# Banded attention inside a gated layer, forward and backward: score and gradient products as 32-row matmuls

## The chip, the cores and the metric

The kernel runs on one core of one Trainium2 chip. The metric is the time of one execution on the device in microseconds, lower is better. The times of before are three runs; the profile is one further execution of the same program, recorded by the hardware profiler. Engines are named as in the profile: PE is TensorE (its weight loads are listed apart, as PEld), DVE is VectorE, ACT is ScalarE, POOL is GpSimd, SP is SyncE, which here only issues transfers.

## The reference

Two branches read the same rows x (2048 x 512, bf16): attention with 32 heads of 16 channels in which each query sees the 256 keys up to its own, and a gated ReLU network of 1376 hidden channels. A sigmoid gate g of x mixes them. The kernel returns the output and the gradients of x and of every weight, for a given gradient of the output.

```python
def _A_ref(x, wqkv, wo):
    H = 32; Dh = D // H; W = 256
    q, k, v = ...                              # (x @ wqkv), split into heads
    scores = einsum("bhqd,bhkd->bhqk", q, k) * (Dh ** -0.5)
    mask = (idx[:, None] - idx[None, :] >= 0) & (idx[:, None] - idx[None, :] < W)
    p = softmax(where(mask, scores, -1e9))
    o = einsum("bhqk,bhkd->bhqd", p, v)
    return o.reshape(B, S, D) @ wo

def _fwd_reference(...):
    g = sigmoid((x * gate_w).sum(-1, keepdims=True))
    return g * _A_ref(x, A_wqkv, A_wo) + (1 - g) * _B_ref(x, B_W_gate, B_W_up, B_W_down)

out, vjp = jax.vjp(f, A_x, A_wqkv, A_wo, B_W_gate, B_W_up, B_W_down, gate_w)
return (out, *vjp(grad_out))
```

## The kernel before

Three stages follow each other. The first (0 to 259 us) makes the gated network's forward and weight gradients; the second (to about 777 us) is the attention, forward and backward; the third makes the output rows and the gradient of x. The change is in the second, with a little preparation in the first.

**Layout.** 512 channels are four column blocks c of 128, so a block has eight heads of 16 channels. 2048 positions are 16 tiles of 128, in four groups of four. For each block and group `project_parts` (L119) makes Q, dO, K and V transposed: channels on the 128 partitions, 512 positions along the row. Q and dO go into the tile `zT` (L136). K and V are each written twice (`K0`, `K1`, `V0`, `V1`, L153 to L160), multiplied by a 0/1 column `par`, so that `K0` keeps the even heads of each pair and has zeros for the odd ones, and `K1` the other way round. A pair of heads is 32 partitions, a strip; a block has four strips.

**The padded operand.** `zt` (L108) holds Q and dO again, as [128, 2, 4 tiles, 4 strips, 128]: for strip k only the partitions 32k to 32k+31 are filled, everything else is zero. It is cleared once at the end of the first stage (L443 to L446) and filled for the first group by eight copies (L145 to L151), later by four transfers per group, `spread` (L468), issued on SP: 64 KB each.

**Units.** A unit (L624 to L640) is one block c, one query tile j, one key tile kb (j, j-1 or j-2: roles d, m, f) and one `half`, which is the parity of the heads it treats, four heads. There are 360. Within a query tile the units of half 0 come first, then those of half 1. The score product ST (`front`, L643, matmul L649) multiplies `K{half}` of the key tile with the four padded copies of the query tile: 128 rows, 128 columns of weights, 512 moving columns, giving four heads' scores with keys on partitions, in one PSUM bank. ACT takes the exponential into `Pu` (L655), POOL masks it by role d or f (L657, L660). The gradient product dPT (`front_dp`, L663, matmul L669) does the same with `V{half}` and dO. DVE multiplies `Pu` with dPT into `Pd` (`gradp`, L671, L674).

**What follows a unit.** `rowsum` (L676) sums into BA with eight small matmuls; `flip` (L694) transposes `Pu` and `Pd`, either by a transfer on SP (159 units, their pair is the tile `PP`) or by eight PE transposes into a PSUM tile `pt` (L706) that ACT and DVE copy out in turn (L72, L74; 201 units). `cd_piece` (L480) uses the flipped tiles for the gradients of K and V (L488, L491). `small_ops` (L711) gives POOL seven small products per query tile.

**Order.** The loop at L821 writes the order out by hand; the framework adds the waits but moves nothing. In step n: POOL's small products; `front` of unit n (ST, exponential, mask); `gradp` of unit n-1; transposing transfers of n-2; `rowsum` and `flip` of n-3; `front_dp` of unit n; pieces of CD; then at most one piece of background, a part of the next group's projection (`prq`) or of the previous block's weight gradients (`bgq`, `grad_parts`, L557), if a running `credit` allows. The credit grows per step by `SLOT` less fixed charges (L872).

**PSUM.** Eight banks: tag "M" has four for ST, dPT, projection sums `pp` and weight-gradient sums `wps`; "TR" two for transposes; one each for CD and BA. A `wps` sum keeps its bank over four background pieces (`held`).

Of the kernel before, what the change touches and what calls it, by code (L numbers as in the profile page):

```python
# [22 lines left out]
def kernel(  # L23
# [21 lines left out]
    P = 128  # L45
# [67 lines left out]
    if True:  # L113
# [5 lines left out]
        def project_parts(c, tg):  # L119
# [4 lines left out]
            def mm(nm, which, eng):  # L124
                ps, tag, bufs, _ = pools["now"]
                pp = ps.tile([P, TGW], F32, tag=tag, bufs=bufs, name="pp")
# [7 lines left out]
                if nm in ("Q", "dO"):  # L134
                    if nm == "Q":
                        t4["z"] = pjA.tile([P, 2, TGW], BF, tag="zT", name="zT")  # L136
                    dst = t4["z"][:, ("Q", "dO").index(nm), :]
                else:
                    dst = pjA.tile([P, TGW], BF, tag="T", bufs=2, name=f"{nm}T")[:]
# [4 lines left out]
                t4[nm] = dst  # L144
                if nm in ("Q", "dO"):  # L145
                    if c == 0 and tg == 0:
                        w = ("Q", "dO").index(nm)
                        for k in range(NP):
                            rows = slice(32 * k, 32 * k + 32)
                            evac(zt[0][rows, w, :, k, :], dst[rows, :].rearrange("p (k q) -> p k q", k=TPG),  # L150
                                 (("dve", "act")[w] if k % 2 else "dve"))  # L151
                else:
                    for k in range(2):  # L153
                        t4[f"{nm}{k}"] = pj.tile([P, TGW], BF, tag=f"{nm}{k}", name=f"{nm}{k}")
                        if PENG[k] == "act":
                            nc.scalar.mul(t4[f"{nm}{k}"][:], pp[:], par[:, k:k + 1])
                        elif PENG[k] == "dve":
                            nc.vector.tensor_scalar(t4[f"{nm}{k}"][:], pp[:], par[:, k:k + 1], None, op0=ALU.mult)
                        else:
                            nc.vector.tensor_scalar(t4[f"{nm}{k}"][:], dst[:], par[:, k:k + 1], None, op0=ALU.mult)  # L160

            def tr(a_nm, b_nm):
                ps, tag, bufs, trt = pools["now"]
                pt = ps.tile([P, 2, TPG, P], BF, tag=trt, bufs=2, name="ptp")
                for a, nm in enumerate((a_nm, b_nm)):
                    for k in range(TPG):
                        nc.tensor.transpose(pt[:, a, k, :], t4[nm][:, k * P:(k + 1) * P], ident[:])
                return pt
# [20 lines left out]
    with ExitStack() as p1, tc.manual_schedule():  # L189
# [209 lines left out]
        DA0 = 2 * NTG  # L399
        pools["now"] = (ps1, "tr", 2, "tr")  # L400
        first = []
        turn_x(0)
        stores = {}
        for n in range(N1 + 8):
# [36 lines left out]
            if n == NTG + 1:  # L441
                nc.scalar.activation(tiny[:], tiny[:], ACT.Exp)
            if t in (NT + 3, NT + 5):  # L443
                i = (t - NT - 3) // 2
                nc.gpsimd.memset(zt[i][:, 0, :, :, :], 0.0)
                nc.vector.memset(zt[i][:, 1, :, :, :], 0.0)  # L446
            if n == N1 - 2:
# [11 lines left out]
    if True:  # L459
# [6 lines left out]
        ps = pps.enter_context(tc.tile_pool(name="attps", bufs=2, space=PSUM))  # L466
        pools["now"] = (ps, "M", 4, "TR")
        def spread(gi, k):  # L468
            rows = slice(32 * k, 32 * k + 32)
            nc.sync.dma_start(zt[gi % ZB][rows, :, :, k, :],  # L470
                              proj[groups[gi]]["z"][rows, :, :].rearrange("p w (k q) -> p w k q", k=TPG))

        P2 = {}
# [6 lines left out]
        def cd_piece(c, kb, qb, half, last):  # L480
# [5 lines left out]
            for hh in range(HH):  # L486
                h = 2 * hh + half
                nc.tensor.matmul(cd[0][:, h, :], lhsT=p2[:, 0, hh, :], rhs=rq[:, h, 0:2 * Dh],  # L488
# [51 lines left out]
        def load_wo():  # L540
            t = pjA.tile([P, 2, TGW], BF, tag="zT", name="wo_z")
            for k in range(2):
                load_rows("wo", A_wo, k, t[:, k, :])
            for k in range(2, DC):
                load_rows("wo", A_wo, k, pjA.tile([P, TGW], BF, tag="T", bufs=2, name="wo_t")[:])
# [11 lines left out]
        def grad_parts(c, rest=None):  # L557
# [22 lines left out]
            def piece(part, t0, first, last):  # L580
                if first:
                    tag, bufs = ("TR", 2) if part == DC and rest is not None else ("M", 4)
                    hold[part] = ps.tile([P, 3, P] if part < DC else [P, D], F32, tag=tag, bufs=bufs, name="wps")
                wps = hold[part]
                for t in range(t0, t0 + 4):
                    go_, no_ = first and t == t0, last and t == t0 + 3
                    if part < DC:
                        nc.tensor.matmul(wps[:], lhsT=x_r[:, t, part * P:(part + 1) * P], rhs=sts[c][:, t, 0:3, :],  # L588
                                         start=go_, stop=no_)
                    else:  # L590
                        nc.tensor.matmul(wps[:], lhsT=sts[c][:, t, 3, :], rhs=rows[t], start=go_, stop=no_)
                if not last:
                    return None
                if part < DC:
                    ws = (gwp if rest is None else S2["t6"]).tile([P, 3, P], BF, tag="ws", bufs=2 if rest is None else 5, name="ws")
                    evac(ws[:], wps[:], "act" if rest is None or part % 2 else "dve")
                    return store(part, ws)
                if t0 + 4 < NT:
                    hold["half"] = gwp.tile([P, D], F32, tag="half", bufs=1, name="half")
                    evac(hold["half"][:], wps[:], "act")  # L600
                    for k in range(4, 8):
# [3 lines left out]
                if "half" in hold:  # L605
                    nc.vector.tensor_tensor(out=ws[:], in0=hold["half"][:], in1=wps[:], op=ALU.add)
                else:
                    evac(ws[:], wps[:], "act")
                return store(part, ws)
# [31 lines left out]
        NU = len(units)  # L641

        def front(u):  # L643
            tg, jl = u.j // TPG, u.j % TPG
            z = zt[(u.c * NTG + tg) % ZB]
            KTt = proj[(u.c, u.kb // TPG)][f"K{u.half}"]
            ksl = slice((u.kb % TPG) * P, (u.kb % TPG + 1) * P)
            ST = ps.tile([P, HH, P], F32, tag="M", bufs=4, name="ST")
            nc.tensor.matmul(ST[:], lhsT=KTt[:, ksl], rhs=z[:, 0, jl, :, :], start=True, stop=True)  # L649
            if u.dma or u.role == "d":  # L650
                u.PP = wk.tile([P, 2, HH, P], BF, tag="PP", bufs=5, name="PP")
                u.Pu, u.Pd = u.PP[:, 0, :, :], u.PP[:, 1, :, :]
            else:
                u.Pu = wk.tile([P, HH, P], BF, tag="Pu", bufs=3, name="Pu")
            nc.scalar.activation(u.Pu[:], ST[:], ACT.Exp)  # L655
            if u.role == "d":
# [5 lines left out]

        def front_dp(u):  # L663
            tg, jl = u.j // TPG, u.j % TPG
            z = zt[(u.c * NTG + tg) % ZB]
            VTt = proj[(u.c, u.kb // TPG)][f"V{u.half}"]
            ksl = slice((u.kb % TPG) * P, (u.kb % TPG + 1) * P)
            u.dPT = ps.tile([P, HH, P], F32, tag="M", bufs=4, name="dPT")
            nc.tensor.matmul(u.dPT[:], lhsT=VTt[:, ksl], rhs=z[:, 1, jl, :, :], start=True, stop=True)  # L669

        def gradp(u):  # L671
            if u.role != "d" and not u.dma:
                u.Pd = wk.tile([P, HH, P], BF, tag="Pd", bufs=3, name="Pd")
            nc.vector.tensor_tensor(out=u.Pd[:], in0=u.Pu[:], in1=u.dPT[:], op=ALU.mult)  # L674

        def rowsum(u):  # L676
# [4 lines left out]
            for hh in range(HH):  # L681
                h = 2 * hh + u.half
                nc.tensor.matmul(BA[:, h, 0:33], lhsT=u.Pu[:, hh, :], rhs=kv[:, u.kb % TPG, h, 1:34],  # L683
# [10 lines left out]
        def flip(u):  # L694
# [7 lines left out]
            copier["i"] += 1  # L702
            pt = ps.tile([P, 2, HH, P], BF, tag="TR", name="pt")
            for a, src in enumerate((u.Pu, u.Pd)):
# [95 lines left out]
        with tc.manual_schedule():  # L800
# [4 lines left out]
            credit = 1.2  # L805
            SLOT = 1.5
            LAG = 3
# [13 lines left out]
            while n <= NU + LAG or ev or cdq or bgq:  # L821
# [5 lines left out]
                if u is not None:  # L827
# [13 lines left out]
                    if u.first and u.j == TPG - 1 and u.c > 0:  # L841
                        bgq += ready
                    front(u)
                    if u.last and gi + 1 == len(groups) and u.j % TPG in (1, 3):
# [8 lines left out]
                if LAG <= n < NU + LAG:  # L853
# [4 lines left out]
                    if w.last:  # L858
# [5 lines left out]
                        for kb in done:  # L864
                            qbs = range(kb, min(NT, kb + 3))
                            for qb in qbs:
                                for half in range(2):
                                    e = n + 1 if qb < w.j else n + 5
                                    cdq.append((e, w.c, kb, qb, half, qb == qbs[-1] and half == 1))
                if u is not None:  # L870
                    front_dp(u)
                credit += SLOT - 0.63 - (0.44 if LAG <= n < NU + LAG and not units[n - LAG].dma else 0.0)  # L872
                for _ in range(2 if len(cdq) > 6 or (len(cdq) > 1 and cdq[1][5] and cdq[1][0] <= n and cdq[1][2] < NT - 1) else 1):
# [13 lines left out]
                elif prq and not held and (credit > 0.4 or due - n <= len(prq)):  # L887
                    credit -= (0.44, 0.86, 0.86, 0.1, 0.86, 0.86)[len(prq) - 1]
                    prq.pop(0)()
                    if len(prq) == 4:  # L890
                        for k in range(NP):
                            ev.setdefault(n + 1 + k // 2, []).append(("dma", lambda gi=gi, k=k: spread(gi + 1, k)))
                    if not prq:
# [134 lines left out]
```

## Time and profile before

| | us |
|---|---|
| median of three runs | 968.75 (966.98 to 973.46) |
| the profiled execution | 971.04 |
| its span, first to last instruction | 969.0 |
| granted TensorE clock, share of full speed | 0.994 |

Busy times over the span, with the number of instructions:

| engine | busy us | share | instructions |
|---|---|---|---|
| PE | 938.9 | 97% | 11281 |
| PEld | 598.3 | 62% | 11281 |
| DVE | 501.5 | 52% | 918 |
| ACT | 473.8 | 49% | 811 |
| POOL | 488.4 | 50% | 936 |

The groups that the change touches, as busy us in all and mean ns of one:

| line | what | count | busy us | mean ns |
|---|---|---|---|---|
| L649 | score product ST on PE | 360 | 136.8 | 380 |
| L669 | gradient product dPT on PE | 360 | 137.2 | 381 |
| L655 | exponential on ACT (both tiles) | 360 | 217.3 | 597 to 657 |
| L657, L660 | mask on POOL | 240 | 152.3 | 634 |
| L674 | product Pd on DVE (both tiles) | 360 | 245.0 | 681 |
| L706 | transposes into pt on PE | 1608 | 156.1 | 220 |
| L72 | copy of pt on ACT | 103 | 105.1 | 1020 |
| L74 | copy of pt on DVE | 102 | 69.5 | 681 |

Busy times of PE are the union of records that overlap, so a mean times a count is more than the busy time. The share over the whole span is an average over three stages. "Idle before" of a group is time in which its engine stood still ahead of it, with what ended the wait.

### The profile page before, as it was taken

The numbers are of one execution on the slowest core, as the hardware profiler recorded it, in microseconds if no ns is written. First come the engines' busy times: TensorE is split into PE (matmuls) and PEld (weight loads), VectorE is DVE, ScalarE is ACT, GpSimd is POOL, SyncE is SP. The second block draws the span as 40 slices with busy tenths as digits, with TensorE's granted clock in tenths as the row PEclk, the third lists the DMA queues.
The fourth block names the chain that finished last, engine by engine and source line by source line (L and its number), as shares of the span: only waits on it lengthen the run. The fifth ranks groups of instructions, "written<-read, shape, count | busy, mean of one in ns | idle before, by whom it ended". The sixth has DMA issues, their size and how long they took to land.

```text
span 969.0 us, 27638 instructions
## 1 busy us (share of the span) xinstructions
PE 938.9 (97%) x11281; PEld 598.3 (62%) x11281; DVE 501.5 (52%) x918; ACT 473.8 (49%) x811; POOL 488.4 (50%) x936
## 2 busy tenths in 40 slices
PE   7999999999999999999999999989999999999998
PEld 4556555656567777676776677756777754444443
DVE  4443323323377777666776667765667613223322
ACT  5422322222378777667776667766677720001001
POOL 2644345444177667666676556665657622121211
PEclk9999999999999999999999999998999999999999
DMA  9988899996667598985889857899999969866760
GB/s 291 185 201 206 218 218 210 220 196 174 143 114 122 100 160 155 154 146 100 145 126 189 138 103 139 127 162 175 160 141 229 185 184 260 194 171 165 183 155 28
DMA packets 447415, 161.64 MB, mean 167 GB/s; under 512 B 365784, under 2 KB 444984, under 8 KB 447288
## 3 DMA queue, kind: packets, MB, share of 16 engines
q1 hardware_dynamic: 424888, 136.80, 73.8%
q10 hardware_dynamic: 20592, 17.84, 6.1%
q0 software_dynamic: 1808, 5.24, 1.5%
q8 instruction: 88, 1.44, 0.7%
q14 instruction: 39, 0.32, 0.1%
HBM read 38.44 MB, written 38.41 MB: 79 GB/s over the span
## 4 chain that ended last, share of the span: by engine, by line
PE 82%; DMA 6%; POOL 4%; SPq 2%; DVE 2%; ACT 1%; issue 1%; ACTq 0%; POOLq 0%; DVEq 0%
PE pt L706 9%; PE dxps L970 8%; PE ST L649 7%; PE dPT L669 7%; PE wps L373 6%; PE wps L588 4%; PE dxps L991 4%; PE BA L683 4%; PE pp L129 4%; PE bps L941 4%; PE CD L488 4%; PE dhps L326 3%; PE ups L326 3%; PE dps L375 3%; PE gps L326 3%; PE CD L491 2%
## 5 line engine op out<-in xcount | busy, mean ns | idle before, releaser
L674 DVE TENSOR_TENSOR Pd<-Pu,dPT 128x512 bf16<-128x512 bf16 x201 | 136.6, 681 | 64.9 <-POOL Pu L660 53.5
L655 ACT ACTIVATE Pu<-ST 128x512 bf16<-128x512 f32 x201 | 121.6, 606 | 58.9 <-PE ST L649 57.3
L649 PE MATMUL ST<-z,K 128*128 128x512 bf16 x360 | 136.8, 380 | 4.0 <-DVE Pd L674 1.7
L669 PE MATMUL dPT<-z,V 128*128 128x512 bf16 x360 | 137.2, 381 | 1.3 <-DVE Pd L674 1.1
L674 DVE TENSOR_TENSOR PP<-PP,dPT 128x512 bf16<-128x512 bf16 x159 | 108.4, 682 | 41.0 <-POOL PP L657 38.1
L657 POOL TENSOR_SCALAR_AFFINE_SELECT PP<-PP 128x512 bf16<-128x512 bf16 x128 | 81.3, 635 | 79.5 <-ACT PP L655 78.8
L655 ACT ACTIVATE PP<-ST 128x512 bf16<-128x512 f32 x159 | 95.7, 602 | 51.7 <-PE ST L649 42.0
L340 POOL TENSOR_TENSOR hT<-rg,upm 128x512 bf16<-128x512 bf16 x44 | 52.2, 1186 | 123.9 <-DVE upm L338 98.4
L488 PE MATMUL CD<-rq,p 128*128 128x32 bf16 x1440 | 109.7, 177 | 0.8 <-ACT rows_st L494 0.5
L373 PE MATMUL wps<-dgu_r,x_r 128*128 128x256 bf16 x704 | 105.6, 272 | 4.9 <-DVE wst L74 4.9
L491 PEld LDWEIGHTS <-p 128*128 128x128 bf16 x1440 | 86.4, 96 | 35.9 <-issue 3.1
L72 ACT COPY p<-pt 128x1024 bf16<-128x1024 bf16 x103 | 105.1, 1020 | 5.2 <-PE pt L706 2.5
L491 PE MATMUL CD<-rq,p 128*128 128x16 bf16 x1440 | 106.7, 169 | 0.0
L488 PEld LDWEIGHTS <-p 128*128 128x128 bf16 x1440 | 99.0, 96 | 1.7 <-issue 1.5
L660 POOL TENSOR_SCALAR_AFFINE_SELECT Pu<-Pu 128x512 bf16<-128x512 bf16 x112 | 71.0, 634 | 41.8 <-ACT Pu L655 40.1
L373 PEld LDWEIGHTS <-x_r 128*128 128x128 bf16 x704 | 68.8, 98 | 36.7 <-issue 6.3
L948 ACT COPY a_sb<-aps 128x512 f32<-128x512 f32 x16 | 9.4, 585 | 145.8 <-issue 133.1
L706 PE MATMUL pt<-ident,Pd 128*128 128x128 bf16 x804 | 78.4, 220 | 0.0
L706 PE MATMUL pt<-ident,Pu 128*128 128x128 bf16 x804 | 77.7, 219 | 0.0
L74 DVE COPY p<-pt 128x1024 bf16<-128x1024 bf16 x102 | 69.5, 681 | 6.1 <-PE pt L706 5.4
L332 ACT ACTIVATE rg<-gps 128x512 bf16<-128x512 f32 x44 | 26.3, 598 | 91.0 <-PE gps L326 49.6
L683 PE MATMUL BA<-KV,Pu 128*128 128x33 bf16 x804 | 66.6, 178 | 4.1 <-ACT BAs L689 4.0
(158 smaller groups left out, 1998.7 us busy)
## 6 DMA issues: line engine op xcount, KB each, us to landing
dqkvo_d<-rows_st SPq DMA_DIRECT2D x7, 1024.0 KB, 5.7
dar<-da_d SPq DMA_DIRECT2D x28, 256.0 KB, 4.3
hT_d<-hT ACTq DMA_DIRECT2D x44, 128.0 KB, 2.4
dgT_d<-dgu ACTq DMA_DIRECT2D x44, 128.0 KB, 2.8
duT_d<-dgu ACTq DMA_DIRECT2D x44, 128.0 KB, 2.8
duT_g<-duT_d SPq DMA_DIRECT2D x8, 640.0 KB, 5.2
dgT_g<-dgT_d SPq DMA_DIRECT2D x7, 640.0 KB, 9.1
gt<-hT_d SPq DMA_DIRECT2D x7, 640.0 KB, 5.7
```

The lines of the kernel that those rows point to most:

```text
L72: nc.scalar.copy(out, in_)
L326: nc.tensor.matmul(out[:], lhsT=w(c), rhs=x(c), start=(c == 0), stop=(c == DC - 1))
L373: nc.tensor.matmul(acc["w"][:, c, :], lhsT=x_r[:, t, c * P:(c + 1) * P], rhs=k.dgu_r[:, :, i, :], start=(go_ and c % 2 == 0), stop=no_, sk ...
L488: nc.tensor.matmul(cd[0][:, h, :], lhsT=p2[:, 0, hh, :], rhs=rq[:, h, 0:2 * Dh], start=cd[1], stop=True, skip_group_check=True)
L491: nc.tensor.matmul(cd[0][:, h, 0:Dh], lhsT=p2[:, 1, hh, :], rhs=rq[:, h, 2 * Dh:3 * Dh], start=False, stop=True, skip_group_check=True)
L649: nc.tensor.matmul(ST[:], lhsT=KTt[:, ksl], rhs=z[:, 0, jl, :, :], start=True, stop=True)
L655: nc.scalar.activation(u.Pu[:], ST[:], ACT.Exp)
L657: nc.gpsimd.affine_select(out=u.Pu[:], in_=u.Pu[:], compare_op=ALU.is_ge, fill=0.0, base=0, pattern=[[0, HH], [1, P]], channel_multiplier=-1)
L669: nc.tensor.matmul(u.dPT[:], lhsT=VTt[:, ksl], rhs=z[:, 1, jl, :, :], start=True, stop=True)
L674: nc.vector.tensor_tensor(out=u.Pd[:], in0=u.Pu[:], in1=u.dPT[:], op=ALU.mult)
L683: nc.tensor.matmul(BA[:, h, 0:33], lhsT=u.Pu[:, hh, :], rhs=kv[:, u.kb % TPG, h, 1:34], start=(u.first and hh == 0), stop=True, skip_group ...
L706: nc.tensor.transpose(pt[:, a, hh, :], src[:, hh, :], ident[:])
```

## The change

Unit, half and strip get another meaning: `half` now names two neighbouring strips (partitions 0 to 63 or 64 to 127 of a block) in place of the parity, so that head `2*hh + half` becomes `HH*half + hh` in `rowsum` and `cd_piece`. A unit's scores are four matmuls of 32 rows, two strips by two parities, each 128 moving columns; so are its gradients. The moving operand is `zT` itself, unpadded. The scores of unit n and the gradients of unit n-1 are written together at the head of step n, strip by strip, and `front_dp` at the end of the step is gone. Scores and gradients of one unit share one PSUM tile `SD` of two banks, one bank per strip: within a bank two quarters hold scores and two hold gradients. There are two such tiles, in the place of the four banks of "M". The projection and weight-gradient sums move to the two banks of the transposes, now called "tr" (the last block's weight gradients, after the loop of units, go in pairs into "M"). `spread`, the padding, the clearing and the first copies are gone; `zT` has two buffers. `SLOT` is 1.4 in place of 1.5, and the fixed charge of the products 0.53 in place of 0.63.

```diff
-                        t4["z"] = pjA.tile([P, 2, TGW], BF, tag="zT", name="zT")
+                        t4["z"] = pjA.tile([P, 2, TGW], BF, tag="zT", bufs=2, name="zT")
...
-                if nm in ("Q", "dO"):
-                    if c == 0 and tg == 0:
-                        w = ("Q", "dO").index(nm)
-                        for k in range(NP):
-                            rows = slice(32 * k, 32 * k + 32)
-                            evac(zt[0][rows, w, :, k, :], dst[rows, :].rearrange("p (k q) -> p k q", k=TPG),
-                                 (("dve", "act")[w] if k % 2 else "dve"))
-                else:
+                if nm in ("K", "V"):
...
-        pools["now"] = (ps, "M", 4, "TR")
-        def spread(gi, k):
-            rows = slice(32 * k, 32 * k + 32)
-            nc.sync.dma_start(zt[gi % ZB][rows, :, :, k, :],
-                              proj[groups[gi]]["z"][rows, :, :].rearrange("p w (k q) -> p w k q", k=TPG))
-
+        pools["now"] = (ps, "tr", 2)
...
-                h = 2 * hh + half
+                h = HH * half + hh
...
-                if first:
-                    tag, bufs = ("TR", 2) if part == DC and rest is not None else ("M", 4)
-                    hold[part] = ps.tile([P, 3, P] if part < DC else [P, D], F32, tag=tag, bufs=bufs, name="wps")
+                if first and rest is not None and part < DC:
+                    if part % 2 == 0:
+                        hold["two"] = ps.tile([P, 2, TGW], F32, tag="M", bufs=2, name="wps")
+                    hold[part] = hold["two"][:, part % 2, 0:3 * P].rearrange("p (a n) -> p a n", a=3)
+                elif first:
+                    hold[part] = ps.tile([P, 3, P] if part < DC else [P, D], F32, tag="tr", bufs=2, name="wps")[:]
...
+        def score(u, nm, w, at, par):
+            tg, jl = u.j // TPG, u.j % TPG
+            lhs = proj[(u.c, u.kb // TPG)][f"{nm}{par}"]
+            z = proj[(u.c, tg)]["z"]
+            ksl = slice((u.kb % TPG) * P, (u.kb % TPG + 1) * P)
+            return [lambda i=i: nc.tensor.matmul(u.SD[:, i, at + par, :], lhsT=lhs[32 * (2 * u.half + i):32 * (2 * u.half + i) + 32, ksl],
+                                                 rhs=z[32 * (2 * u.half + i):32 * (2 * u.half + i) + 32, w, jl * P:(jl + 1) * P],
+                                                 start=True, stop=True, skip_group_check=True) for i in range(2)]
+
+        def products(u, v):
+            if u is not None:
+                u.SD = ps.tile([P, 2, 4, P], F32, tag="M", bufs=2, name="SD")
+            for par in range(2):
+                for f in (score(v, "V", 1, 2, par) if v is not None else []) + (score(u, "K", 0, 0, par) if u is not None else []):
+                    f()
+
         def front(u):
...
-            ST = ps.tile([P, HH, P], F32, tag="M", bufs=4, name="ST")
-            nc.tensor.matmul(ST[:], lhsT=KTt[:, ksl], rhs=z[:, 0, jl, :, :], start=True, stop=True)
...
-            nc.scalar.activation(u.Pu[:], ST[:], ACT.Exp)
+            nc.scalar.activation(u.Pu[:].rearrange("p (i r) q -> p i (r q)", i=2), u.SD[:, :, 0:2, :].rearrange("p i r q -> p i (r q)"), ACT.Exp)
...
-        def front_dp(u):
...
-            u.dPT = ps.tile([P, HH, P], F32, tag="M", bufs=4, name="dPT")
-            nc.tensor.matmul(u.dPT[:], lhsT=VTt[:, ksl], rhs=z[:, 1, jl, :, :], start=True, stop=True)
...
-            nc.vector.tensor_tensor(out=u.Pd[:], in0=u.Pu[:], in1=u.dPT[:], op=ALU.mult)
+            flat = lambda a: a.rearrange("p (i r) q -> p i (r q)", i=2)
+            nc.vector.tensor_tensor(out=flat(u.Pd[:]), in0=flat(u.Pu[:]), in1=u.SD[:, :, 2:4, :].rearrange("p i r q -> p i (r q)"), op=ALU.mult)
...
-            pt = ps.tile([P, 2, HH, P], BF, tag="TR", name="pt")
+            pt = ps.tile([P, 2, HH, P], BF, tag="tr", bufs=2, name="pt")
...
-            SLOT = 1.5
+            SLOT = 1.4
...
+                if n <= NU:
+                    products(u, units[n - 1] if n >= 1 else None)
+                if u is not None:
                     front(u)
...
-                if u is not None:
-                    front_dp(u)
-                credit += SLOT - 0.63 - (0.44 if LAG <= n < NU + LAG and not units[n - LAG].dma else 0.0)
+                credit += SLOT - 0.53 - (0.44 if LAG <= n < NU + LAG and not units[n - LAG].dma else 0.0)
...
-                    if len(prq) == 4:
-                        for k in range(NP):
-                            ev.setdefault(n + 1 + k // 2, []).append(("dma", lambda gi=gi, k=k: spread(gi + 1, k)))
```

More of the change, by code (lines that the diff above doesn't have):

```diff
@@ L124, in mm @@
             def mm(nm, which, eng):
-                ps, tag, bufs, _ = pools["now"]
+                ps, tag, bufs = pools["now"]
                 pp = ps.tile([P, TGW], F32, tag=tag, bufs=bufs, name="pp")
@@ L162, in tr @@
             def tr(a_nm, b_nm):
-                ps, tag, bufs, trt = pools["now"]
-                pt = ps.tile([P, 2, TPG, P], BF, tag=trt, bufs=2, name="ptp")
+                ps, _, _ = pools["now"]
+                pt = ps.tile([P, 2, TPG, P], BF, tag="tr", bufs=2, name="ptp")
                 for a, nm in enumerate((a_nm, b_nm)):
@@ L399 @@
         DA0 = 2 * NTG
-        pools["now"] = (ps1, "tr", 2, "tr")
+        pools["now"] = (ps1, "tr", 2)
         first = []
@@ L442 @@
                 nc.scalar.activation(tiny[:], tiny[:], ACT.Exp)
[L443 to L446, printed above, removed]
             if n == N1 - 2:
@@ L540, in load_wo @@
         def load_wo():
-            t = pjA.tile([P, 2, TGW], BF, tag="zT", name="wo_z")
+            t = pjA.tile([P, 2, TGW], BF, tag="zT", bufs=2, name="wo_z")
             for k in range(2):
@@ L587, in piece @@
                     if part < DC:
-                        nc.tensor.matmul(wps[:], lhsT=x_r[:, t, part * P:(part + 1) * P], rhs=sts[c][:, t, 0:3, :],
+                        nc.tensor.matmul(wps, lhsT=x_r[:, t, part * P:(part + 1) * P], rhs=sts[c][:, t, 0:3, :],
                                          start=go_, stop=no_)
                     else:
-                        nc.tensor.matmul(wps[:], lhsT=sts[c][:, t, 3, :], rhs=rows[t], start=go_, stop=no_)
+                        nc.tensor.matmul(wps, lhsT=sts[c][:, t, 3, :], rhs=rows[t], start=go_, stop=no_)
                 if not last:
@@ L595, in piece @@
                     ws = (gwp if rest is None else S2["t6"]).tile([P, 3, P], BF, tag="ws", bufs=2 if rest is None else 5, name="ws")
-                    evac(ws[:], wps[:], "act" if rest is None or part % 2 else "dve")
+                    evac(ws[:], wps, "act" if rest is None or part % 2 else "dve")
                     return store(part, ws)
@@ L599, in piece @@
                     hold["half"] = gwp.tile([P, D], F32, tag="half", bufs=1, name="half")
-                    evac(hold["half"][:], wps[:], "act")
+                    evac(hold["half"][:], wps, "act")
                     for k in range(4, 8):
@@ L605, in piece @@
                 if "half" in hold:
-                    nc.vector.tensor_tensor(out=ws[:], in0=hold["half"][:], in1=wps[:], op=ALU.add)
+                    nc.vector.tensor_tensor(out=ws[:], in0=hold["half"][:], in1=wps, op=ALU.add)
                 else:
-                    evac(ws[:], wps[:], "act")
+                    evac(ws[:], wps, "act")
                 return store(part, ws)
@@ L641 @@
         NU = len(units)
-        def front(u):
[L644 to L647, printed above, removed]
-            ST = ps.tile([P, HH, P], F32, tag="M", bufs=4, name="ST")
-            nc.tensor.matmul(ST[:], lhsT=KTt[:, ksl], rhs=z[:, 0, jl, :, :], start=True, stop=True)
+        def score(u, nm, w, at, par):
[12 more added lines that the diff above has]
+                    f()
+        def front(u):
             if u.dma or u.role == "d":
@@ L661, in front @@
                                         pattern=[[0, HH], [-1, P]], channel_multiplier=1)
-        def front_dp(u):
[L664 to L667, printed above, removed]
-            u.dPT = ps.tile([P, HH, P], F32, tag="M", bufs=4, name="dPT")
-            nc.tensor.matmul(u.dPT[:], lhsT=VTt[:, ksl], rhs=z[:, 1, jl, :, :], start=True, stop=True)
         def gradp(u):
@@ L681, in rowsum @@
             for hh in range(HH):
-                h = 2 * hh + u.half
+                h = HH * u.half + hh
                 nc.tensor.matmul(BA[:, h, 0:33], lhsT=u.Pu[:, hh, :], rhs=kv[:, u.kb % TPG, h, 1:34],
```

## The prediction

> **What bounds the kernel now.** I read the page first: the busy slices, to find the stretch that the change touches; then the busy times of that stretch alone, the order of TensorE's instructions inside it, and last who waits for whom there.
>
> ```profile
> span 969.0 us, 27638 instructions
> ...
> PE   7999999999999999999999999989999999999998
> PEld 4556555656567777676776677756777754444443
> DVE  4443323323377777666776667765667613223322
> ACT  5422322222378777667776667766677720001001
> ```
>
> A slice is 24.2 us. ACT and DVE rise together from slice 10 to 32: that is the attention loop. The first score product starts at 258.97 us and the 360th at 772.93, so a step (one unit) lasts 513.96/359 = 1.43 us. Stages before and after contain nothing that the edit makes shorter, so the 517 us up to the last gradient product decide.
>
> ```profile
> 259.00:779.00 520.00, 506.27 (x8652) 361.51 (x8653) 357.02 (x649) 371.10 (x633) 337.98 (x783) 0.99 0.84 147
> ```
>
> Columns: stretch, its length, busy us and instructions of PE, PEld, DVE, ACT, POOL, granted clock, DMA share, GB/s. TensorE shows 97%; the others sit at 65 to 71%. A busy TensorE may still be waiting in a pipeline, so I looked at starts.
>
> ```profile
> 455.15 0.38 PE L669 MATMUL dPT<-z,V 128*128 128x512 bf16 x1
> 455.36 0.18 PE L488 MATMUL CD<-rq,p 128*128 128x32 bf16 x1
> 455.39 0.17 PE L491 MATMUL CD<-rq,p 128*128 128x16 bf16 x1
> ...
> 455.98 0.38 PE L706 MATMUL pt<-ident,Pu 128*128 128x128 bf16 x4
> 456.20 0.39 PE L706 MATMUL pt<-ident,Pd 128*128 128x128 bf16 x4
> 456.42 0.38 PE L669 MATMUL dPT<-z,V 128*128 128x512 bf16 x1
> ```
>
> A record lasts longer than its place in the queue. The 512-column product holds the engine 0.21 us, four 128-column ones 0.22 (0.055 each), a 32- or 16-column one 0.025. Summing start to start against these, only about 28 of the 517 us are idle: TensorE's own work sets the pace, some 1.36 of 1.43 us a step, and ST with dPT is 2 x 0.215 = 0.43 of it (155 us in all).
>
> ```profile
> ACT Pu L655 <- PE ST L649: 57.3, 101, 1.3
> DVE Pd L674 <- POOL Pu L660: 53.5, 66, 1.7
> ACT PP L655 <- PE ST L649: 42.0, 73, 1.9
> POOL Pu L660 <- ACT Pu L655: 40.1, 53, 1.6
> DVE PP L674 <- POOL PP L657: 38.1, 64, 1.7
> ```
>
> These are waits in the same stretch (total us, times, longest). They show a chain score, exponential, mask, product, each engine waiting for the one before. Today it costs TensorE almost nothing: ST waited for Pd 1.7 us in total, in seven places.
>
> **Part by part.** *Products on TensorE.* Removed per unit: two of 0.215. Added: eight of 128 columns, each over 32 rows. No matmul of 32 rows is in this trace. If two row groups run side by side: 4 x 0.055 = 0.22. (Neighbouring units are of the same half four times in six, and then use only two of the four row groups.) If they run one after another: 8 x 0.055 = 0.44. The start-to-start floor, 8 x 0.025 = 0.20, is lower than both. Each step also changes from 128-row to 32-row work and back. Nothing here shows that; at worst the array empties each time, which costs the overlap that records show now: 0.17 lasting, 0.025 to the next start, so 0.145, twice 0.29. Ends: 0.20 and 0.44 + 0.29 = 0.73; the gain is between +0.23 and -0.30 a step (-83 to +108 us over 360). I take side by side with part of the change-over exposed, between 0.22 and 0.51: 0.33, nearer the low end, since weights of all other products load beside the running one (0.096 records, 0.025 apart). Gain 0.10 x 360 = 36 us.
>
> [...]
>
> *PSUM and the loop it closes.* Before, ST and dPT each took one of four banks and ST(n+2) waited only for the exponential of n. Now a unit owns one two-bank tile, and there are two. Scores of n+2 need the tile of n, free only after the product Pd(n) on DVE. So two steps cannot be shorter than the chain from ST to the end of Pd. In the trace that takes 2.83 us median, 3.00 mean; two steps are 2.86 mean. Its floor for a masked unit (240 of 360): start to exponential 0.41, exponential 0.60, hand-over 0.07, mask 0.63, hand-over 0.03, Pd 0.69, hand-over back 0.04: 2.48 us. The other 0.56 of the mean (3.04 with the last hand-over) is queueing behind copies on ACT (1.02 each), small products on POOL (0.40 each) and copies on DVE (0.68).
>
> Steps are uneven, so averages don't suffice. I took the 358 two-step distances between ST starts, less 2 x 0.10. 144 of them are below 2.48, by 57 us in sum; below 2.76 (half the queueing left) 182, by 105 us. One wait lengthens two overlapping distances, so I count half: 28 to 52 us. When TensorE waits, the queues empty, so I take a quarter of the queueing left (2.62): 40 us. What would make this cheaper is Pd starting sooner. What makes it dearer: the gradient products of n move from the end of step n to the head of step n+1, and with scores and gradients of a unit in one bank I take it that they must wait for the exponential's read. 92 of 359 exponentials today end after the next ST starts. Behind a waiting product stand the next scores, row sums, transposes and background, all of TensorE. The floor of that wait (0.41 + 0.60 + 0.04 = 1.05 us a step) would bind 110 steps by 16 us; nearly all of it lies in the short pairs already counted, so I add nothing for it.
>
> *The "tr" pair of banks.* Projection and weight-gradient sums move there from "M", beside the flips' transposes. A held weight sum leaves the flips one bank. Three blocks have 42 gaps between pieces of one sum; pieces stand some 1.7 us apart (400.20, 402.13, 403.62 in the chain), 72 us in all. In that time 201 x 72/517 = 28 flips come, 14 copied by ACT; each makes the next set of transposes wait some 1.02 + 0.25 - 0.89 = 0.38. Upper end 14 x 0.38 = 5, plus some for projections: I take 6 us. The lower end is 0, where flips don't follow each other.
>
> *Edits at nothing.* The 60 spreads (64 KB each) leave the SP queue:
>
> ```profile
> z<-zT SPq DMA_DIRECT2D x60, 64.0 KB, 2.4
> ```
>
> ST never waited for one by the list of waits, and the transposes behind them on SP waited for engines. The eight first copies and two memset pairs lie beside phase-one matmuls (150 to 240 us, TensorE at 9 tenths). If that cover were gone, the copies would cost 6 x 0.28 + 2 x 0.62 = 2.9 us. Exponential and Pd read the same 512 elements from two banks instead of one: no row differs in that, 0. The background's schedule stays: SLOT and the products' charge both fall by 0.10.
>
> Sum: -36 + 40 + 6 = +10 us on the profiled run (971.04; span 969.0 and 2 around it), 981. The median before is 2.3 lower, so 979.
>
> **The rivals.**
>
> *The queues empty and the products cost 0.22 (faster).* Gain 0.21 x 360 = 76. Against two-step distances less 0.42, the floor 2.48 lacks 94 us, half is 47; "tr" 0. -29: 940 on the median's scale. For it: ACT, DVE and POOL are 30% idle. Against: the five waits above are already floor time. It decides when the chain stays under some 2.5 us.
>
> *Every change of row count empties the array (slower).* Products 0.22 + 0.29 = 0.51: -0.08 x 360 = +29; the longer steps leave the loop 15 (2.62 against distances plus 0.16) and "tr" 6: +50, 1019. [...] The switch happens 720 times; from 0.09 us each the step loses TensorE time.
>
> *The products don't run beside each other.* 8 x 0.055 = 0.44, change-over free: +4, loop 23, "tr" 6: +33, 1001. For it: in this trace every matmul starts after the column count of the one ahead has passed.
>
> **How the numbers follow.** Likeliest 0.42 (own range 963 to 994), queues empty 0.28, emptied array 0.20, one after another 0.10. About 1% is what a measurement of this kernel can tell from no change (968.75: 959.1 to 978.4). The first case lies 0.20 slower, 0.20 within, 0.02 faster; the second 0.27 faster, 0.01 within; the third 0.20 slower; the fourth 0.09 slower, 0.01 within. Faster 0.29, same 0.22, slower 0.49. The range drops the lower third of the second case and the upper half of the third: 936 to 1022.
>
> **What would show it.** Start of a unit's first product to that of the next instruction after its eight: 0.33 expected, 0.22 and 0.51 for the rivals. Waits of TensorE for Pd (DVE) and for the exponential (ACT): 20 to 50 us where there were 3. Distance from scores to the end of Pd near 2.6. Attention steps of 1.46 us. Wrong if TensorE stays without idle time while the step falls, or if TensorE waits elsewhere, on "pt" above all.

## The result, and the profile after

The changed kernel takes 1064.56 us (median of four, 1063.34 to 1066.49), the kernel before 969.42 beside it: a ratio of 1.098, with a 95% interval of 1.094 to 1.102. The forecast was 979 with a range of 936 to 1022. The direction was the likeliest one; the size is 95 us where 10 were forecast.

The granted clock before, slice by slice (tenths of full speed):

```profile
PEclk9999999999999999999999999998999999999999
```

The head of the page of the changed kernel, and from its slices the engines and the granted clock:

```profile
span 1064.8 us, 31836 instructions
...
PE   8999999999898998999998999899999999999998
PEld 5565555555566776666676666676676774444443
DVE  5443222333566565556665566565656541323232
ACT  5422222322566565666665566665666651010111
...
PEclk9999999999688577799876899857999589999999
```

The attention is now slices 10 to 32 of 26.6 us. The last line above is the surprise: the granted clock, at 9 tenths nearly throughout before, lies at 5 to 8 for much of the stage. It switches between full and half, at times that are whole multiples of 3.41 us apart: in the stage the trace has half-clock stretches of 1 to 9 times 3.413 us (the longest from 826.3 to 857.0 us) and full ones of 1 to 18 times between them. The first stage and the last are nearly as long as before (259 and 261 us, 195 and 197 us); the stage from the first score product to the last gradient product went from 514.8 to 606.8 us.

Busy time of the stage, columns as in the prediction (stretch, length, PE, PEld, DVE, ACT, POOL, clock, DMA share, GB/s):

```profile
259.00:870.00 611.00, 562.54 (x10724) 417.51 (x10771) 366.63 (x649) 377.34 (x632) 340.07 (x778) 0.82 0.69 119
```

DVE, ACT and POOL do what they did, in more time. TensorE is still shown 92% busy, at 0.82 of the clock. One block of products between its neighbours, from the timeline of TensorE at full clock:

```profile
501.41 0.81 PE L129 MATMUL pp<-x,p 128*128 128x512 bf16 x3
502.15 0.23 PE L635 MATMUL SD<-zT,V 32*128 32x128 bf16 x2
502.22 0.22 PE L635 MATMUL SD<-zT,K 32*128 32x128 bf16 x2
502.27 0.22 PE L635 MATMUL SD<-zT,V 32*128 32x128 bf16 x2
502.33 0.22 PE L635 MATMUL SD<-zT,K 32*128 32x128 bf16 x2
502.48 0.19 PE L673 MATMUL BA<-KV,PP 128*128 128x33 bf16 x1
```

The two strips run side by side: the two of a pair start mostly 3 to 4 ns apart (99 such blocks at full clock), and the pairs follow at 0.055 us. But the last pair is followed by BA only after 0.147 us instead of 0.055, and over the stage the first product comes 0.08 to 0.10 us later than the matmul ahead of it would allow. Each change of row count costs about 0.09 here. The trace shows this price at both ends; whether the array empties in that time it doesn't show (the last record lasts 0.22 us, and BA starts 0.15 after its start).

Who waits for whom in the stage (us in total, times, longest):

```profile
ACT Pu L652 <- PE SD L635: 101.4, 120, 1.9
...
PEld L635 <- issue: 98.9, 255, 0.9
...
DVE Pd L664 <- PE SD L635: 48.7, 70, 1.5
```

DVE, which waited mostly for POOL's masks before (53.5 us), now waits for products at least as much (48.7, and 41.7 for masks). The list gives TensorE only 36 us of waits for ACT and DVE at the products (20.5, 10.7 and smaller ones), since a stalled product can be seen at the weight load ahead of it, as "issue"; that entry is no measure of stalls either (51 us of it stand in e7 below, where 6 us of gaps lie ahead of products). Counted start to start, gaps over 0.13 us ahead of a product are 76 us: 35 end with an exponential, 33 with a Pd.

### The profile page after: what moved, and what is told of

Read it like the earlier page. It is cut to its first block, busy times and chain, and to the rows that moved or that the text cites. A ratio compares the mean times of both kernels' runs of the same rounds, so it can differ in the third digit from the quotient of the medians.

```text
span 1064.8 us, 31836 instructions
## 1 busy us (share of the span) xinstructions
PE 997.1 (94%) x13344; PEld 657.1 (62%) x13441; DVE 506.2 (48%) x910; ACT 479.2 (45%) x809; POOL 488.4 (46%) x934
## 5 line engine op out<-in xcount | busy, mean ns | idle before, releaser
L664 DVE TENSOR_TENSOR Pd<-Pu,SD 128x512 bf16<-128x512 bf16 x201 | 137.7, 685 | 90.9 <-PE SD L635 48.7
L652 ACT ACTIVATE Pu<-SD 128x512 bf16<-128x512 f32 x201 | 120.9, 602 | 105.1 <-PE SD L635 101.4
L635 PE MATMUL SD<-zT,V 32*128 32x128 bf16 x1440 | 144.7, 243 | 24.5 <-ACT Pu L652 20.5
L635 PE MATMUL SD<-zT,K 32*128 32x128 bf16 x1440 | 133.6, 244 | 17.1 <-DVE Pd L664 10.7
L664 DVE TENSOR_TENSOR PP<-PP,SD 128x512 bf16<-128x512 bf16 x159 | 108.7, 684 | 65.2 <-PE SD L635 38.2
L652 ACT ACTIVATE PP<-SD 128x512 bf16<-128x512 f32 x159 | 95.1, 598 | 75.1 <-PE SD L635 73.9
L635 PEld LDWEIGHTS <-V 32*128 32x128 bf16 x1440 | 72.3, 99 | 85.6 <-issue 73.7
L696 PE MATMUL pt<-ident,Pd 128*128 128x128 bf16 x804 | 96.2, 254 | 0.0
L696 PE MATMUL pt<-ident,Pu 128*128 128x128 bf16 x804 | 92.7, 250 | 0.8 <-ACT p L72 0.6
L635 PEld LDWEIGHTS <-K 32*128 32x128 bf16 x1440 | 74.3, 101 | 28.9 <-issue 25.2
```

The lines of the kernel that those rows point to most:

```text
L635: return [lambda i=i: nc.tensor.matmul(u.SD[:, i, at + par, :], lhsT=lhs[32 * (2 * u.half + i):32 * (2 * u.half + i) + 32, ksl], rhs=z[32 ...
L652: nc.scalar.activation(u.Pu[:].rearrange("p (i r) q -> p i (r q)", i=2), u.SD[:, :, 0:2, :].rearrange("p i r q -> p i (r q)"), ACT.Exp)
L664: nc.vector.tensor_tensor(out=flat(u.Pd[:]), in0=flat(u.Pu[:]), in1=u.SD[:, :, 2:4, :].rearrange("p i r q -> p i (r q)"), op=ALU.mult)
L696: nc.tensor.transpose(pt[:, a, hh, :], src[:, hh, :], ident[:])
```

## The experiments

All times are medians; the kernel before took 969.2 to 970.7 beside them.

**e1, all 128 rows.**

```diff
-  ... lhsT=lhs[32 * (2 * u.half + i):32 * (2 * u.half + i) + 32, ksl], rhs=z[32 * (2 * u.half + i):32 * (2 * u.half + i) + 32, w, jl * P:(jl + 1) * P], ...
+  ... lhsT=lhs[:, ksl], rhs=z[:, w, jl * P:(jl + 1) * P], ...
```

> The changed kernel with each of the eight products over all 128 rows instead of 32 (same tiles, order, waits and PSUM banks; scores and gradients are then sums over four heads, so the attention part is another function). Clock theory (the 32-row products leave the array too sparsely used, the granted clock halves in light stretches, and that is some 69 of the 95 us): granted clock 0.98 or more, time 985 to 1000. Wait theory (the two SD tiles and the shared banks hold TensorE, and the clock falls because of that idle time): clock stays under 0.93, time over 1045. Switch theory (changing between 128 and 32 rows is what costs): time 990 to 1000, but the clock stays under 0.93, since the waits remain.

1033.85 us, ratio 1.066 (1.062 to 1.070). No theory had this pair of numbers: the clock is whole, as the clock theory asked, and the time is far over its 1000. (The products of e1 sum over four heads, so it is a measure of time and not a kernel to use; the same holds for e5, e6, e10, e12 and e13, and in e7 and e11 half of the heads repeat the other half.) The stage in e1, and what TensorE waited for there:

```profile
257.00:836.00 579.00, 525.91 (x10679) 460.75 (x10728) 363.43 (x648) 375.40 (x630) 338.57 (x776) 1.00 0.73 126
```

```profile
PE SD L635 <- ACT Pu L652: 27.4, 62, 0.8
PE SD L635 <- DVE Pd L664: 10.1, 19, 0.8
```

There are no 32-row matmuls, no changes of row count, a full clock, and still 65 us more. Start to start, 79 us of gaps stand ahead of products, 50 of them ending with an exponential. So there are at least two causes.

**e2, an extra matmul per unit.**

```diff
+  nc.tensor.matmul(u.SD[:, 0, 0:2, :], lhsT=ident[:], rhs=proj[(u.c, u.j // TPG)]["z"][:, 0, 0:2 * P], start=True, stop=True, skip_group_check=True)
```

> The changed kernel with one more 128-row matmul of 256 columns per unit, into the scores' own bank ahead of the scores, which overwrite it; 0.11 us x 360 = 38 us more work for TensorE. Clock theory: the granted clock rises to 0.95 or more and the kernel gets faster in spite of it, 1030 to 1055. Wait and switch theories: clock about 0.89 as it is, time 1090 to 1105.

1069.84 us. The granted clock rose from 0.89 to 0.96 (half-clock time after the first stage from 225 to 79 us), and the added work, by estimate 360 x 0.11 = 38 us (256 columns at half of the 0.215 us of 512), cost 5. That fits a clock that costs time, but the extra matmul also moved the wait for the tile's release ahead of everything (68 us of gaps, ended by Pd), so it settles no size.

**e3, halves side by side.** The unit list runs over `half` inside the key tiles.

> The changed kernel with the two halves of a key tile as neighbouring units, so that scores of one unit and gradients of the last stand on different strips and all four row groups work. Block of eight products 0.42 to about 0.31 us at full clock. Clock theory: the clock falls below 0.88, since the array is used still less, and the time stays at 1050 to 1090. Wait and switch theories: 0.1 x 360 = 36 us faster, 1025 to 1040, clock as it is.

1104.29 us, clock 0.89: outside every expectation. The block did fall to 0.223 us after its start (0.327 before), and the kernel got 40 us slower. Gaps ahead of products grew to 143 us, of which 80 end with an exponential and 52 with a Pd. What TensorE saved in the block came back as waits, and more. The order of masked and unmasked units changed with it, so this is not a clean measure of the row groups.

**e4, gradients at the end of the step.**

```diff
...
+                if u is not None:
+                    for q in range(2):
+                        for f in score(u, "V", 1, 2, q):
+                            f()
                 credit += SLOT - 0.53 ...
```

> The changed kernel with the gradient products back at the end of the unit's own step: two more changes of row count per step, and each block has two row groups of two. Switch and clock theories: 0.2 us more a step at full clock, 1120 to 1160, clock under 0.89. Wait theory (the wait of the gradients for the exponential at the head of the step is the loss): about the same or faster, 1040 to 1075.

1215.25 us, clock 0.84: beyond every theory. Besides two more changes per step, the gradients of a unit now wait for the exponential of the same unit: 114 us of gaps end with one. Moving the gradients away from the head of the step did not remove their wait, as the wait theory had it, but brought it forward. The result mixes two causes and settles neither.

**e5, scores and gradients in different banks of the tile.**

```diff
-  ... u.SD[:, i, at + par, :], ...
+  ... u.SD[:, at // 2, 2 * i + par, :], ...
...
```

> e1_full_rows with the scores of a unit in one bank of its tile and its gradients in the other (128-row products, sums over four heads as there). Gradients then need not wait for the exponential's read; the tile is still released by Pd. If the shared bank is the loss: 50 us less, 980 to 990. If the release by Pd takes its place: 1005 to 1034, with some 60 us of TensorE's waits now for DVE.

1034.81 us, as e1, and the waits are the same to about a microsecond: 50 us of gaps end with an exponential, 28 with a Pd (27 in e1). The edit did not take the wait away: the order between uses of one tile holds even when the banks differ. It says nothing about the bank.

**e6, a tile for the scores and one for the gradients.**

```diff
-  u.SD = ps.tile([P, 2, 4, P], F32, tag="M", bufs=2, name="SD")
+  u.ST = ps.tile([P, HH, P], F32, tag="M", bufs=2, name="ST")
+  v.dPT = ps.tile([P, HH, P], F32, tag="MD", bufs=2, name="dPT")
...
```

> e1_full_rows with a one-bank tile of two buffers for the scores and another for the gradients, each released by its own reader, as before the change (sums over four heads as there). Still changed against the kernel before: the head-of-step order, 128-column pieces, no spreads, projection and weight-gradient sums in the transposes' banks. Theory that the pair tile is the loss: 965 to 985. Theory that the shared transposes' banks or the order hold TensorE: over 1000.

970.58 us, ratio 1.0005 (0.9988 to 1.0021). TensorE's waits there:

```profile
PE CD L472 <- ACT rows_st L478: 2.5, 6, 0.9
PE dPT L633 <- DVE Pd L664: 2.1, 7, 0.5
```

So e6 to e1, the pair tile alone, is 63 us. The shared banks for transposes, the new order in the step and the missing spreads together cost or gain nothing that can be measured. (With 8 x 0.055 = 0.44 the products cost nearly what they did before, 0.43.)

**e12 and e13, one wait at a time.** Both are e6 with a copy of one element: on DVE out of the scores' tile behind Pd, or on ACT into the gradients' tile behind the exponential.

> e6_own_tiles with one more DVE copy of a single element of the scores' tile after Pd, so that the scores' tile is released only when Pd has ended, as in the pair tile; the gradients need not wait for the exponential (sums over four heads as in e6). If the release by Pd alone is the loss of e1: 1015 to 1040, with TensorE waiting for DVE at the scores. If the gradients' wait for the exponential is the loss: 965 to 985 (the small copies take DVE time beside TensorE).

> e6_own_tiles with an ACT copy of a single element into the gradients' tile right behind the exponential, so that the gradient products at the head of the next step wait for the exponential as in the pair tile, while the scores' tile is still released by the exponential (sums over four heads as in e6; the copy's element is overwritten). If the wait for the exponential alone is the loss of e1: 1010 to 1040 (the copies also load ACT). If the release by Pd is: 968 to 990.

1029.05 us (ratio 1.060, 1.056 to 1.063) and 1021.98 us (1.054, 1.050 to 1.058). TensorE's longest waits, first of e12, then of e13:

```profile
PE ST L633 <- DVE tiny L665: 39.6, 99, 0.9
```

```profile
PE dPT L633 <- ACT dPT L652: 35.2, 80, 0.9
```

Either wait alone gives 51 to 58 us, both together 63. They replace each other. Each copy lies in the chain and takes 0.14 us itself, so both numbers are too high by an amount that was not measured.

**e7, 32 rows without the pair tile.** e6 with `lhs` and `z` cut to 32 rows, the same ones for both strips.

> e6_own_tiles with every product over 32 rows of one row group per unit, so none run beside each other (both strips take the first strip's rows, so half of the heads repeat the other half). It adds two changes of row count per step and takes the row count down, with the waits gone and the same 8 x 0.055 us streaming. If a change costs 0.1 and the clock looks at streaming time alone: e6 plus 65 to 80 us, clock 0.97 or more. If the clock counts rows: clock under 0.93 and e6 plus more than 90 us. If a change is free: within 15 us of e6.

1049.94 us, 79 above e6, clock 0.93: at the edge of two expectations. The stage of e6 and then that of e7 are the clearest pair of lines of this study:

```profile
258.00:775.00 517.00, 505.93 (x10777) 452.26 (x10778) 359.31 (x649) 373.37 (x633) 337.74 (x778) 1.00 0.84 138
258.00:854.00 596.00, 593.46 (x10741) 463.27 (x10741) 362.00 (x647) 375.82 (x629) 339.64 (x778) 0.87 0.70 122
```

In e7 TensorE is 99.6% busy, its list of waits in the stage adds up to 2 us, and its clock is 0.87.

**e8, the extra matmul in light steps alone** (209 of 360, 22 us of work by the same estimate).

> The changed kernel with the extra 128-row matmul of 256 columns of e2 only in steps after one that had no background piece (projection or weight gradient), about half of the 360: at most 20 us more work for TensorE. If the lowered clock costs time of its own, beside the waits: granted clock 0.95 or more and 1040 to 1058, below the changed kernel's 1064.6. If the lowered clock only fills time that TensorE would have waited anyway: 1064 to 1085 with the same clock.

1067.23 us (ratio 1.098, 1.093 to 1.103), clock 0.93: the time fits the second expectation, the clock lies between the two. Half-clock time fell from 225 to 145 us and the total did not; like e2 it brings its own wait (56 us of gaps ended by Pd). Inconclusive.

**e9, e10, e11, wider small matmuls.** The matmuls of CD and the first of BA take 0.025 us from start to start with 16 columns as with 33, and 0.026 when they are widened to 56. e9 does this to the changed kernel, e10 to e6, e11 to e7. The extra columns add into their neighbours, so these three measure time and compute other gradients.

```diff
-  nc.tensor.matmul(cd[0][:, h, :], lhsT=p2[:, 0, hh, :], rhs=rq[:, h, 0:2 * Dh],
+  nc.tensor.matmul(wide(cd[0], h * 2 * Dh), lhsT=p2[:, 0, hh, :], rhs=wide(rq, h * 3 * Dh),
...
```

> The changed kernel with the small matmuls of CD (32 and 16 columns) and the first of BA (33) widened to 56 columns, which still fit in the 0.025 us that each takes, so that the array does more at no time (row sums and the gradients of K and V become another function: the extra columns add into their neighbours). Nothing of the products, waits or changes of row count is touched. If the clock follows rows times columns per window of 3.41 us, with the edge near 0.37 of the full rate: granted clock 0.98 or more. If the lowered clock is what stands between e1 (1034) and the changed kernel (1065): 1015 to 1038. If it only fills time that TensorE would have waited: over 1055.

> The control: e6_own_tiles with the same widened matmuls (same change of function, and sums over four heads as in e6). If the widening is free: 965 to 976, as e6. If 56 columns cost more than 0.025 us: 12 matmuls a step are dearer and e9 has to be read with that.

> e7_own_tiles_32 (32-row products one after another, no new waits) with the same widened matmuls. Two changes of row count per step by the starts in e7's trace: 0.09 to 0.19 us a step, with the clock back at 0.98 or more: 1035 to 1045 if the price of e7 is the changes alone at 0.19 x 360 = 68, below 1010 if it was mostly the clock.

e9 takes 1021.17 us (1021.12 to 1031.64; ratio 1.055, 1.046 to 1.063), e10 973.32 (1.003, 1.001 to 1.005), e11 1013.69 (1.043, 1.039 to 1.047). Clock of e9, slice by slice, in its profiled and slowest run:

```profile
PEclk9999999999889999899998999898999999999999
```

More multiplications at the same places make the changed kernel 43 us faster and e7 36 us faster. The clock was 0.97 to 0.985 in e9 and 0.986 to 0.99 in e11, at the lower edge of what was expected or a little under it in e9. The control is 3 us dearer than e6, so the widening is nearly free. The waits are not what changed: the gaps ahead of products are 76 us in e9 as in the changed kernel, while the half-clock time after the first stage fell from 225 to 56 us.

**The rule behind it.** For each 3.41 us window of the attention I added up rows x columns of the matmuls that start in it, as a share of what 128 rows and back-to-back columns (512 in 0.215 us) would give, and asked whether a share under 0.37 tells that the next window runs at half clock. Beside it stands the same with columns alone, where two matmuls that stream side by side count once and the edge is the best one for all kernels together, 0.41.

| kernel | windows | next at half clock | wrong, rows x columns | wrong, columns |
|---|---|---|---|---|
| before | 151 | 3 | 0 | 0 |
| changed | 178 | 66 | 7 | 23 |
| e2 | 180 | 23 | 5 | 9 |
| e3 | 191 | 72 | 4 | 13 |
| e4 | 221 | 111 | 15 | 18 |
| e7 | 174 | 44 | 4 | 39 |
| e8 | 179 | 42 | 5 | 6 |
| e9 | 168 | 16 | 3 | 10 |
| e11 | 163 | 6 | 0 | 5 |
| e1, e6 | 169, 150 | 0 | 0, 0 | 0, 1 |

The edge was found in the runs up to e8 and stood in the expectation of e9, so e9 and e11 are tests of it. With its own best edge columns alone still miss 10 in e7. How much a 32-row matmul counts can be varied: in full, the 1924 windows of the table give 164 misses at the best edge, as a half 75, as a quarter 43, as an eighth 39. So it counts far less than its columns; a quarter, its share of the rows, is consistent with that, and an eighth would be too. The length of the window is that of the shortest stretches at half clock in the traces of before and of the changed kernel, 3.413 us. Idle time alone does not tell the two levels apart: e1 has 79 us of gaps ahead of products and no window at half clock, e7 has 2 us of waits in the stage and 44. Why 7 windows of the changed kernel and 15 of e4 go against the rule is open.

**The sum.**

| from, to | what differs | us |
|---|---|---|
| e6 970.6, e1 1033.9 | the pair tile | +63 |
| e1 1033.9, e9 1021.2 | 32-row products, two changes a step, clock nearly whole, wider small matmuls | -13 |
| e9 1021.2, changed 1064.6 | the lowered clock | +43 |

The middle row is near to what the trace gives: a block lasts 0.327 us, or 0.223 where neighbours are of different halves (two steps in six), 0.29 on average, plus 0.095 ahead of it: 0.39 against the 0.44 of e1, 0.05 x 360 = 18 us, of which the widening takes back 3. The 43 us are what e9 won back and not the whole price of the clock, since e9 still has 56 us at half clock. None of the kernels tried is faster than the one before.

## Why the prediction was wrong

*What bounds the kernel.* Right: TensorE's own work set the pace, and the loop of score, exponential, mask and product was the thing to watch.

*Products: 0.33, a gain of 36 us.* Mis-sized. Side by side, until then the author's assumption, was right, and 0.327 is what a block with equal halves lasts; that it meets the 0.33 is luck, because the 0.33 was to hold the change-over at both ends, and the 0.095 ahead of the block comes on top. Against the 0.43 of before the trace leaves 0.04 a step, a gain of 15 us.

*The loop: 40 us.* The mechanism was right, the size too small, for two choices. First, a quarter of the queueing was to be left when TensorE waits. From the first score to the end of Pd the changed kernel takes 2.95 us on average, 3.00 before; with the hand-over of 0.04 and less the floor of 2.48 that leaves 0.51 of 0.56, nine tenths. The rule of counting half the missing time would have been good: with all the queueing (3.04) and no gain on the products it gives 123/2 = 61 us, and the pair tile cost 63 from e6 to e1. Second, the gradients' wait for the exponential was put at nothing because it would lie inside pairs already counted. e13 has it at up to 51 us by itself; it is true that it adds little to the other (63 with both).

*"tr": 6 us.* e6 shows no cost that can be measured, so the lower end, 0.

*Edits at nothing.* Right as far as e6 shows: with the spreads, copies and padding gone it is at the time of before.

*The step that failed.* The sum had no term for the clock, which put it at nothing without a reason; at least 43 of the 86 us between 979 and 1064.6 are that. The loop adds 23 (63 where 40 stood), the products 21 (a gain of 15 where 36 stood), and "tr" takes 6 off, 81 in all. The row was in front of me: a granted clock of 0.994, taken as given. In the kernel before it fell twice in the attention, at 653.5 and 755.9 us, beside waits of TensorE of 2.9 and 2.3 us that ended at 655.3 and 754.9 us, a hint that it follows the work in a window. The change takes products from 2 x 512 columns over 128 rows to a quarter of the row-columns, and the bill of what the array would then be doing was not made: before, no window of the attention that kept its clock had a share under 0.47; after it, the windows ahead of a drop have 0.24 to 0.40.

*The rivals.* "Every change of row count empties the array" had a cost at the right place: a change takes 0.09 at either end, not 0.145, and whether the array empties is not shown. From e10 to e11, with products serial in four steps of six, it is 40 us. "One after another" was wrong, as was "queues empty". No rival held the clock; with it in none of the cases, nothing pushed the range beyond 1022.

## What to carry to other kernels

Before an edit makes a busy TensorE's work smaller, add up rows x columns per 3.41 us window: below some 0.37 of the full rate the clock halved in these kernels, and a column of "busy" at 99% does not show it. Ask of a merged PSUM tile who reads it last: two readers that released two tiles at two times now release one tile at the later time, and every use of it is ordered; here that cost 63 us (e6 to e1), four times what the products saved (15). When a loop over engines is to become the bound, take its traced length with all its queueing, not its floor.

## What the runs showed of the hardware

- The granted clock followed rows x columns per window of 3.413 us (43 misses in 1924 windows at the edge of 0.37), not busy time: in the attention stage e7 at 99.6% busy has 0.87, e1 at 91% busy and with 79 us of gaps has 1.00.
- Matmuls of 16 to 33 columns widened to 56, at 0.025 and 0.026 us each, made the changed kernel 43 us faster (e9), and e7 36 us faster (e11).
- A change between 128-row and 32-row matmuls costs about 0.095 us going in and 0.09 coming out, at full clock (changed kernel, e11).
- Products on two row groups of one strip each start mostly 3 to 4 ns apart, and pairs follow at 0.055 us; with four row groups a block of eight is followed by the next matmul 0.223 us after its start (changed kernel, e3).
